# Twenty second-layer products of a fused Mamba-2 and ELU-MLP kernel done in halves of 128 tokens

## The chip, the cores and the metric

The kernel runs on one core of a Trainium2 chip. Its time is in device microseconds, the median of three runs; a profiled execution of its own gives the trace. Instructions run on five engines: PE (TensorE, matrix products; PEld is its weight loads), DVE (VectorE), ACT (ScalarE), POOL (GpSimd) and SP (SyncE, which here only issues transfers).

## The reference

A Mamba-2 scan in chunks, whose output is a batch of 3072 tokens of 256 numbers, goes through a two-layer MLP with ELU between. Inputs: x (4, 8, 768, 32), a (4, 8, 768), B and C (4, 8, 768, 16); the weights w_in (256, 2048) and w_out (2048, 256) are float64 arrays, the output is float32.

```
# scan, for each batch, head and chunk of 32 tokens (state: 16 x 32)
cum = cumsum(log(a));  M = (C B^T) * exp(cum_i - cum_j) * (i >= j)
y   = M x + exp(cum) * (C state)
state = exp(sum log a) * state + sum_j exp(cum_last - cum_j) B_j x_j
# bridge: heads side by side, 3072 tokens x 256
h = x @ w_in
g = where(h > 0, h, exp(min(h, 0)) - 1)
out = g @ w_out
```

## The kernel before, in words

The tokens are cut into 12 blocks (`n` = 0 to 11) of 256 (`BLK`), so that two neighbours, n and n+1 with n even, are the same stretch of two batches. The kernel works with chunks of 64 tokens (`Q`). The whole schedule is written out by hand: every engine carries out its instructions in the order in which the code issues them, and the loops at the end of the kernel interleave three kinds of work on PE.

The scan of a block consists of many small products in 32- or 64-wide corners of the array. `scores` (L532, C times B) and `sums` (L562, the sums for the states) stand one behind the other; some time later come `across` (L607, what the state at the start of a chunk gives) and `inside` (L626, M times x). For blocks 4 to 11 the scans of two blocks are issued together, so that `scores` and `sums` of a pair come as one run of small products and `across` and `inside` as another. `end_of_two` issues `across` and `inside` for blocks 4/5, 6/7, 8/9 and 10/11. The results of `inside` are copied out as yT, which feeds the first layer. `scan_ahead` and `turn_step` issue the scan's other parts: loads, exponentials, transposes.

The first layer of a pair of blocks (`front`, `mid`, `back`, all through `part_product`, L730) makes seven products in place of eight by a Strassen-like scheme on quarters of w_in, with sums on DVE (L747, L755, L763). Blocks 0 to 3 are done plainly (`l1`, L658). `elu` (L671, L678, L680) turns the results into g.

The second layer of blocks 0 and 1 is plain (`l2`, L779). For the pairs from 2/3 on `second(n)` makes seven products too. It is a generator: its caller draws some products at a time (`l2s`), between the first-layer products of the next pair. The 2048 hidden numbers are taken in two halves of four chunks; in each half r runs over the seven products, and for each r four products of a 128x128 weight quarter with a 128x256 piece of g add up in one PSUM tile (L869). DVE, ACT and POOL then add the tile to the parts of the output (`add`, L841; copies L875, L889; differences through `sub`, L795). For the last pair (`last`), g is the stationary operand and each product is done as two of 128 columns (L864); those of r = 6 in its second half stand at L849.

`second(4)`, for blocks 4 and 5, is drawn while the first layer of blocks 6 and 7 runs. After it come, in PE's order, `scores` and `sums` of blocks 8/9, `across` and `inside` of 8/9, then both for 10/11.

A product of float32 operands written as one in the code is two weight loads and two matmuls in the trace.

Of the kernel before, what the change touches and what calls it, by code (L numbers as in the profile page):

```python
# [16 lines left out]
P = 128  # L17
Q = 64
BLK = 2 * P
# [9 lines left out]
def kernel(  # L29
# [27 lines left out]
    nc = tc.nc  # L57
# [21 lines left out]
    def psum(shape, name):  # L79
        return p_a.tile(shape, F32, tag="a", name=name)  # L80
# [6 lines left out]
    for k in range(4):  # L87
        (nc.scalar if k % 2 else nc.sync).dma_start(
            out=la0[BH * k:BH * (k + 1)],
# [181 lines left out]
    for v in range(2):  # L271
        nc.gpsimd.affine_select(
            out=low16[Q * v:Q * v + Q], in_=low16[Q * v:Q * v + Q], pattern=[[1, Q]],
# [5 lines left out]
        out=hmask, in_=hmask, pattern=[[-N, NH]], compare_op=ALU.is_ge, fill=0.0,  # L279
        base=0, channel_multiplier=1)  # L280
    nc.gpsimd.affine_select(
        out=hmask, in_=hmask, pattern=[[N, NH]], compare_op=ALU.is_ge, fill=0.0,
# [8 lines left out]
        out=minus, in0=ident, scalar1=-1.0, scalar2=None, op0=ALU.mult)  # L291
# [474 lines left out]
    def row_of(n):  # L766
        b, g = place(n)
        return b * S + g * BLK
# [25 lines left out]
    def sub(out, in0, in1):  # L794
        nc.gpsimd.tensor_tensor(out=out, in0=in0, in1=in1, op=ALU.subtract)  # L795

    def quarters(n, i):


        A, B = g_of[n, i], g_of[n + 1, i]  # L800
        if n < 4:
            return A[:, 0], A[:, 1], B[:, 0], B[:, 1]
        return A[:, 0], B[:, 0], B[:, 1], A[:, 1]
# [5 lines left out]
    def sum_t2(n, half):  # L809
        for i in range(4 * half, 4 * half + 4):  # L810
            t2_of[n, i] = ffn.tile([P, BLK], F32, tag="t2", name="t2", bufs=4)
            b11, b21, b12, b22 = quarters(n, i)
            sub(t2_of[n, i], b22, b12)
# [3 lines left out]
    def second(n, last=False):  # L817


        c = c_of[n] = ffn.tile([P, 2, 2, 2, P], F32, tag="c", name="c_sum", bufs=1)  # L820
        c11, c12, c21, c22 = (
            c[:, at, :, e] if last else c[:, at, e] for e in range(2) for at in range(2))

        def finish(e, at):
            if last:
                return
            if (n, at) not in turned_of:
                turned_of[n, at] = conv.tile([P, 2, BLK], F32, tag="sgn", name="turned")
            nc.vector.transpose(
                out=turned_of[n, at][:, e], in_=c[:, at, e].rearrange("p t c -> p (t c)"))  # L830

        a11, a12, s1, a22 = a_out
        s2, s3, s4 = s_out
        for half in range(2):
            tmp = ffn.tile([P, 3, 2, P], F32, tag="tmp", name="p_sum", bufs=1)
            p1, p5, u = (tmp[:, r] for r in range(3))
            chunk = range(4 * half, 4 * half + 4)

            def add(out, in0, in1):
                eng = nc.vector if in0.tensor is ps.tensor else nc.gpsimd  # L840
                eng.tensor_tensor(out=out, in0=in0, in1=in1, op=ALU.add)  # L841

            for r, a in enumerate((a11, a12, s1, s2, s3, a22, s4)):
                if last and half and r == 6:
                    store(n, 0)
                    for ts, queue in enumerate((nc.scalar, nc.sync)):
                        ps = psum([P, P], "ps_o")
                        for i in chunk:
                            nc.tensor.matmul(  # L849
                                out=ps, lhsT=quarters(n, i)[3][:, ts * P:(ts + 1) * P],  # L850
                                rhs=a[:, i], start=(i == chunk[0]), stop=(i == chunk[-1]))
                        nc.vector.tensor_tensor(
                            out=c12[:, ts], in0=ps, in1=c12[:, ts], op=ALU.add)
                        r0 = row_of(n + 1) + ts * P
                        queue.dma_start(out=out[r0:r0 + P, 0:P], in_=c12[:, ts])
                    return
                pool, tag = (p_a, "a") if (7 * half + r) % 2 else (p_o, "o")
                ps = pool.tile([P, 2, P], F32, tag=tag, name="ps_o")
                for i in chunk:
                    b11, b21, b12, b22 = quarters(n, i)  # L860
                    b = (b11, b21, b12, t2_of[n, i], b11, b21, b22)[r]
                    if last:
                        for ts in range(2):
                            nc.tensor.matmul(  # L864
                                out=ps[:, ts], lhsT=b[:, ts * P:(ts + 1) * P], rhs=a[:, i],
                                start=(i == chunk[0] and ts == 0), stop=(i == chunk[-1]),
                                skip_group_check=True)
                    else:
                        nc.tensor.matmul(  # L869
                            out=ps.rearrange("p t c -> p (t c)"), lhsT=a[:, i], rhs=b,  # L870
                            start=(i == chunk[0]), stop=(i == chunk[-1]))
                    if i < chunk[-1]:
                        yield
                if r == 0:
                    nc.scalar.copy(out=p1, in_=ps)  # L875
                    for i in chunk:
                        b11 = quarters(n, i)[0]
                        sub(b11, t2_of[n, i], b11)
                    if half:
                        add(c11, c11, p1)  # L880
                elif r == 1:
                    add(c11, ps, c11 if half else p1)
                    if half:
                        finish(0, 0)
                    for i in chunk:
                        b21 = quarters(n, i)[1]
                        sub(b21, b21, t2_of[n, i])
                elif r == 2:
                    nc.scalar.copy(out=p5, in_=ps)  # L889
                elif r == 3:  # L890
                    add(u, ps, p1)
                    add(p5, p5, u)
                    if half:
                        add(c22, c22, p5)
                        add(c12, c12, p5)
                elif r == 4:
                    add(c22, ps, c22 if half else p5)
                    add(u, ps, u)
                    if half:
                        finish(1, 1)  # L900
                    if half:
                        add(c21, c21, u)
                    if last and half:
                        r0 = row_of(n + 1)
                        nc.sync.dma_start(
                            out=out[r0:r0 + BLK, P:2 * P].rearrange("(t p) c -> p t c", p=P),
                            in_=c22)
                    if not half:
                        sum_t2(n, 1)
                    elif n + 2 < NP:  # L910
                        sum_t2(n + 2, 0)
                elif r == 5:
                    add(c21, ps, c21 if half else u)
                    if half:
                        finish(1, 0)
                else:
                    add(c12, ps, c12 if half else p5)
                    if half:
                        finish(0, 1)
                yield  # L920

    def store(n, at):
        r0 = row_of(n + at)
        nc.sync.dma_start(
            out=out[r0:r0 + BLK, :].rearrange("(t p) e -> p t e", p=P),
            in_=c_of[n][:, at].rearrange("p t e c -> p t (e c)"))
# [29 lines left out]
    half = [slice(0, P), slice(P, 2 * P)]  # L956
# [272 lines left out]
    for n in range(4, NP, 2):  # L1229
        m = n + 2 if n + 2 < NP else None  # L1230
        steps = second(n - 2)

        def l2s(count):
# [10 lines left out]
        for k in range(16):  # L1244
            i = k // 2
# [55 lines left out]
    n = NP - 2  # L1301
    for k, _ in enumerate(second(n, True)):
        if k < 4:
            store_turned(n - 2, k // 2, k % 2)
# [30 lines left out]
```

## Time and profile before

| what | value |
| --- | --- |
| timed runs, us | 357.68, 359.85, 360.68; median 359.85 |
| profiled execution, us | 356.04 |
| its span, first to last instruction, us | 354.2 |
| granted TensorE clock, share of full speed | 1.00 |
| PE busy, us | 344.7 (97%) |
| DVE, ACT, POOL busy, us | 244.2, 204.1, 231.4 |
| instruction queue q8 | 28 packets, 0.46 MB |

The span leaves out what lies around the first and the last instruction of the program. A busy share is a mean over stages; PE's is near the whole. "x" and a number behind a group is a number of the trace's records. In lists of waits, "issue" is time in which an engine stood still and waited for nothing that the profile records.

### The profile page before, as it was taken

How to read it: one execution, taken by the hardware profiler on the slowest of the kernel's cores; microseconds unless marked ns; L12 is line 12 of the kernel's file. 1: busy time of each engine (PE TensorE's matmuls, PEld its weight loads, DVE VectorE, ACT ScalarE, POOL GpSimd, SP SyncE). 2: the span in 40 equal slices, each digit the busy share in tenths (PEclk: the TensorE clock that was granted, in tenths of full speed). 3: DMA queues.
4: the chain of work that ended last, by engine and by line, in shares of the span. 5: the costliest groups of instructions: out<-in, count | busy, mean ns of one | idle time of the engine just before them, and what ended most of it. 6: DMA issues, size and time to landing. Idle time of an engine off the chain costs nothing.

```text
span 354.2 us, 9156 instructions
## 1 busy us (share of the span) xinstructions
PE 344.7 (97%) x3510; PEld 297.0 (84%) x3510; DVE 244.2 (69%) x513; ACT 204.1 (58%) x497; POOL 231.4 (65%) x366
## 2 busy tenths in 40 slices
PE   8899999999999999999999998999998999999996
PEld 5679888888888888888888886888886888888996
DVE  4998978963999677776687774777683666567212
ACT  4789988886345567545666534577635443535100
POOL 5654555544486996985485986377786455455883
PEclk9999999999999999999999999999999999999999
DMA  8968997462351400267300268200000200000102
GB/s 152 270 172 204 291 219 173 115 100 43 69 130 38 84 1 0 34 132 144 55 0 2 31 129 158 45 3 0 7 9 5 44 2 0 0 17 15 32 0 61
DMA packets 87955, 26.45 MB, mean 75 GB/s; under 512 B 75048, under 2 KB 82792, under 8 KB 87912
## 3 DMA queue, kind: packets, MB, share of 16 engines
q1 hardware_dynamic: 85592, 25.60, 33.1%
q10 hardware_dynamic: 2320, 0.26, 0.5%
q8 instruction: 28, 0.46, 0.5%
q14 instruction: 15, 0.12, 0.1%
HBM read 22.51 MB, written 3.34 MB: 73 GB/s over the span
## 4 chain that ended last, share of the span: by engine, by line
PE 87%; DVE 3%; SPq 2%; issue 2%; POOL 2%; DMA 2%; ACT 1%; DVEq 0%; POOLq 0%; ACTq 0%
PE ps_h L730 26%; PE ps_o L869 25%; PE ps_h L658 15%; PE ps_o L779 8%; PE ps_o L864 7%; PE ps_y L626 2%; DMA w<-in_moe_w_in_dram 2%; PE ps_y L607 1%; PE ps_g L532 1%; PE ps_st L562 1%; POOL g L795 1%; SPq L169 1%; DVE g L680 1%; PE ps_o L849 1%; SPq L134 0%
## 5 line engine op out<-in xcount | busy, mean ns | idle before, releaser
L671 ACT ACTIVATE e<-ps_h 128x512 f32<-128x512 f32 x96 | 57.1, 594 | 90.4 <-DVE ps_h L755 48.5
L680 DVE SCALAR_TENSOR_TENSOR g<-e,ps_h 128x512 f32<-128x512 f32 x96 | 65.0, 679 | 13.9 <-ACT e L678 13.6
L869 PE MATMUL ps_o<-g,w_out 128*128 128x256 f32 x256 | 64.2, 380 | 0.0
L658 PE MATMUL ps_h<-yT,w_in 128*128 128x256 f32 (+1 forms) x272 | 60.4, 370 | 1.8 <-POOL w_in L239 1.8
L678 ACT ACTIVATE e<-e 128x512 f32<-128x512 f32 x96 | 61.0, 635 | 2.0
L807 POOL TENSOR_TENSOR g<-g 128x256 f32<-128x256 f32 x33 | 23.9, 726 | 53.8 <-DVE g L680 53.7
L658 PEld LDWEIGHTS ps_h<-yT,w_in 128*128 128x128 f32 x272 | 48.5, 190 | 9.1 <-POOL w_in L239 2.5
L869 PEld LDWEIGHTS ps_o<-g,w_out 128*128 128x128 f32 x256 | 48.4, 190 | 6.7
L512 ACT ACTIVATE L<-L,ncum 128x64 f32<-128x64 f32 x160 | 41.0, 337 | 0.2
L730 PE MATMUL ps_h<-y_sum,w_in 128*128 128x256 f32 x128 | 38.4, 381 | 0.2 <-DVE ps_h L755 0.2
L730 PE MATMUL ps_h<-yT,w_in 128*128 128x256 f32 x128 | 38.4, 381 | 0.0
L730 PE MATMUL ps_h<-y_sum,w_sum 128*128 128x256 f32 x128 | 38.1, 379 | 0.0
L763 DVE TENSOR_TENSOR ps_h<-ps_h,u_sum 128x512 f32<-128x512 f32 x32 | 22.3, 698 | 21.8 <-PE ps_h L730 21.6
L517 POOL TENSOR_SCALAR_AFFINE_SELECT L<-L 64x512 f32<-64x512 f32 x40 | 27.6, 689 | 11.8 <-ACT L L512 9.5
L747 DVE TENSOR_TENSOR u_sum<-ps_h,u_sum 128x512 f32<-128x512 f32 x32 | 22.1, 689 | 17.6 <-ACT u_sum L740 9.6
L869 PE MATMUL ps_o<-g,w_sum 128*128 128x256 f32 x128 | 33.2, 379 | 0.0
L779 PE MATMUL ps_o<-w_out,g 128*128 128x256 f32 x128 | 30.7, 382 | 0.0
L795 POOL TENSOR_TENSOR t<-g 128x256 f32<-128x256 f32 x40 | 28.9, 753 | 0.3
L755 DVE TENSOR_TENSOR ps_h<-ps_h,u_sum 128x256 f32<-128x256 f32 x32 | 13.8, 430 | 22.1 <-PE ps_h L730 22.1
L795 POOL TENSOR_TENSOR g<-g,t 128x256 f32<-128x256 f32 x40 | 28.8, 751 | 0.3
L795 POOL TENSOR_TENSOR g<-t,g 128x256 f32<-128x256 f32 x40 | 27.9, 729 | 1.1 <-PE ps_o L864 1.1
L730 PEld LDWEIGHTS ps_h<-y_sum,w_in 128*128 128x128 f32 x128 | 23.5, 189 | 4.9 <-DVE ps_h L755 1.2
(127 smaller groups left out, 586.1 us busy)
## 6 DMA issues: line engine op xcount, KB each, us to landing
L<-flat SPq DMA_DIRECT2D x20, 256.0 KB
w<-in_moe_w_out_dram SPq DMA_DIRECT2D x8, 512.0 KB
w<-in_moe_w_in_dram SPq DMA_DIRECT2D x7, 512.0 KB
xr<-in_x_dram SPq DMA_DIRECT2D x24, 128.0 KB
out_dram<-turned SPq DMA_DIRECT2D x64, 32.0 KB
bc<-in_B_dram SPq DMA_DIRECT2D x24, 64.0 KB
bc<-in_C_dram SPq DMA_DIRECT2D x22, 64.0 KB
ec<-flat_exp SPq DMA_DIRECT2D x10, 128.0 KB
```

The source lines that it names most:

```text
L512: nc.scalar.activation(L[:, h, u], L[:, h, u], ACT.Exp, bias=ncum[:, u, row:row + 1])
L517: nc.gpsimd.affine_select(out=part, in_=part, pattern=[[0, 4], [0, 2], [1, Q]], compare_op=ALU.is_ge, fill=0.0, base=0, channel_multiplier=-1)
L658: nc.tensor.matmul(out=ps[:, j, toks], lhsT=w_in[:, k, m * P:(m + 1) * P], rhs=yT[n // 2][:, k, n % 2].rearrange("p u i -> p (u i)")[:, toks],
L671: nc.scalar.activation(begun[0], lag[0][2], ACT.Relu, scale=-1.0)
L678: nc.scalar.activation(e, e, ACT.Exp, scale=-1.0)
L680: nc.vector.scalar_tensor_tensor(out=g_of[n, i], in0=e, scalar=1.0, in1=ps, op0=ALU.subtract, op1=ALU.max)
L730: nc.tensor.matmul(out=out, lhsT=lhsT, rhs=rhs, start=first, stop=True, skip_group_check=True)
L779: nc.tensor.matmul(out=o_of[n][:, ts], lhsT=g_of[n, j][:, m % 2, ts * P:(ts + 1) * P], rhs=w_out[:, m], start=(m == 0 and ts == 0), stop=( ...
L795: nc.gpsimd.tensor_tensor(out=out, in0=in0, in1=in1, op=ALU.subtract)
L807: eng.tensor_tensor(out=b12, in0=b12, in1=b11, op=ALU.subtract)
L864: nc.tensor.matmul(out=ps[:, ts], lhsT=b[:, ts * P:(ts + 1) * P], rhs=a[:, i], start=(i == chunk[0] and ts == 0), stop=(i == chunk[-1]), s ...
L869: nc.tensor.matmul(out=ps.rearrange("p t c -> p (t c)"), lhsT=a[:, i], rhs=b, start=(i == chunk[0]), stop=(i == chunk[-1]))
```

## The change

In `second`, for n = 4, in the first half and for r from 0 to 4, each of the four products over 256 token columns is made as two over 128 columns each, with the same weight quarter and into the two halves of the same PSUM tile. These are 20 products, which become 40. The first piece of the first chunk alone has the start flag; the second piece of that chunk has none. All other products pass through the new loop with a single cut that is the whole width.

```
--- before.py
+++ after.py
@@ -866,9 +866,14 @@
                                 start=(i == chunk[0] and ts == 0), stop=(i == chunk[-1]),
                                 skip_group_check=True)
                     else:
-                        nc.tensor.matmul(
-                            out=ps.rearrange("p t c -> p (t c)"), lhsT=a[:, i], rhs=b,
-                            start=(i == chunk[0]), stop=(i == chunk[-1]))
+                        cuts = [slice(0, BLK)]
+                        if n == 4 and not half and r < 5:
+                            cuts = [slice(0, P), slice(P, BLK)]
+                        for cut in cuts:
+                            nc.tensor.matmul(
+                                out=ps.rearrange("p t c -> p (t c)")[:, cut], lhsT=a[:, i],
+                                rhs=b[:, cut], start=(i == chunk[0] and cut.start == 0),
+                                stop=(i == chunk[-1]), skip_group_check=True)
                     if i < chunk[-1]:
                         yield
                 if r == 0:
```

## The prediction

> **What bounds the kernel now.** I read the page first. TensorE (PE) is busy for 97% of the span at the full granted clock and makes 87% of the chain that ended last, so only what shortens PE's own line of work counts. The page also has a queue that carries no data: q8 brings instructions, 28 packets.
>
> ```profile
> span 354.2 us, 9156 instructions
> PE 344.7 (97%) x3510; PEld 297.0 (84%) x3510; DVE 244.2 (69%) x513; ACT 204.1 (58%) x497; POOL 231.4 (65%) x366
> q8 instruction: 28, 0.46, 0.5%
> PE 87%; DVE 3%; SPq 2%; issue 2%; POOL 2%; DMA 2%; ACT 1%; DVEq 0%; POOLq 0%; ACTq 0%
> ```
>
> The list of PE's waits then says what PE lost, in us in total, times, and the longest:
>
> ```profile
> PE ps_y L626 <- issue: 3.1, 2, 1.5
> PE ps_h L658 <- POOL w_in L239: 1.8, 3, 1.0
> PE ps_idle L254 <- DVE idle L249: 1.1, 1, 1.1
> PE ps_h L730 <- DVE ps_h L755: 0.2, 1, 0.2
> PE ps_st L562 <- DVE g L680: 0.2, 1, 0.2
> ```
>
> The largest is not a wait for an engine: twice, inside `inside` (L626), PE stood for 1.5 us with nothing that the profile shows to wait for. PE's timeline places them: the bursts of small products (`across` L607, `inside` L626) of blocks 6/7, of 8/9 and of 10/11 (columns: start us, us, what, and in brackets the idle time before it).
>
> ```profile
> 159.29 0.83 PE L607 MATMUL ps_y<-cts,Sx 32*64 32x64 f32 x48
> 160.05 1.51 PE L626 MATMUL ps_y<-M,xr 64*32 64x64 f32 x128
> 161.49 0.70 PE L730 MATMUL ps_h<-yT,w_in 128*128 128x256 f32 x2
> ...
> 212.97 0.91 PE L607 MATMUL ps_y<-cts,Sx 32*64 32x64 f32 x64
> 213.81 1.37 PE L626 MATMUL ps_y<-M,xr 64*32 64x64 f32 x114
> 216.72 0.34 PE L626 MATMUL ps_y<-M,xr 64*32 64x64 f32 x14 [1.53 <-issue]
> ...
> 268.02 0.91 PE L607 MATMUL ps_y<-cts,Sx 32*64 32x64 f32 x64
> 268.86 1.15 PE L626 MATMUL ps_y<-M,xr 64*32 64x64 f32 x91
> 271.54 0.63 PE L626 MATMUL ps_y<-M,xr 64*32 64x64 f32 x37 [1.54 <-issue]
> ```
>
> The same work runs through in one burst, stops after 114 of 128 matmuls in the next and after 91 in the third: the stop belongs to no fixed place of the work. What it belongs to shows in the transfers. The DMA view of 214.3 to 214.4 us holds one instruction packet, that of 269.1 to 272 us another:
>
> ```profile
> q8 instruction: 1, 0.02, 62.6%
> ...
> q8 instruction: 1, 0.02, 2.1%
> ```
>
> The packet records put their starts at 214.34 and 269.18 us. PE resumes 2.38 and 2.36 us later: it had run out of instructions.
>
> **Where the edges lie.** I number PE's entries of the trace (weight loads, matmuls, recorded semaphore instructions) in order of start: 7116. With 28 packets and 0.46 MB that is about 255 entries and 16 KB a packet. The first late entry is 5058 in the burst of 8/9 and 6081 in that of 10/11; 1023 apart, the packets being the 19th and the 23rd: four blocks of 255.75. So edges lie near 4293, 4548, 4803, 5058, 5314, 5569, 5825, 6081 and 6336, and the packet for one block starts when PE is about one block ahead of it. A burst of `across` and `inside` has 384 entries (96 products, each two weight loads and two matmuls) and takes 2.3 us; wide products take 108 ns an entry, 27 us a block. Only a block that lies wholly in small products can be eaten before the next is there. Before, the bursts are entries 4701 to 5085 and 5770 to 6154: blocks 4803 to 5058 and 5825 to 6081 lie wholly inside them. For blocks 6/7 (3632 to 3984) edges lie near 3528, 3783 and 4038, the last beyond the end, and nothing is lost.
>
> **The change, part by part.** It removes 20 products of 256 columns (first half, r from 0 to 4, chunks 0 to 3, n = 4) and adds 40 of 128. Nothing else differs: the other engines' instructions stand in the same order, no transfer or wait is added, and the accumulations of L841 and the copies of L875 and L889 still start at the last product of a group.
>
> *The split itself.* A wide product is two matmul entries, at 216 ns from start to start; the last stage runs the same products as 128 columns (L864). The chain of waits has both:
>
> ```profile
> 197.15 1.73 PE ps_o L869 x8
> 326.32 23.23 PE ps_o L864 x208
> ```
>
> 1.73/8 = 0.216 us, so 0.432 per wide product; 23.23/208 = 0.1117, so 4 x 0.1117 = 0.447 per pair. 20 x 0.015 = +0.30 us, on PE's path, as PE has no idle time from 163 to 182 us where they run. Less than nothing is excluded: the same columns stream. The dear bound is a weight load that hides behind nothing:
>
> ```profile
> L869 PEld LDWEIGHTS ps_o<-g,w_out 128*128 128x128 f32 x256 | 48.4, 190 | 6.7
> ```
>
> At 190 ns for each of four entries it is 20 x (0.760 - 0.432) = +6.6 us. I take 0.30, since L864 is the same product in the same form.
>
> *The shift.* 40 products for 20 are 80 more entries ahead of all later work. The edges stay; the bursts move to 4781 to 5165 and 5850 to 6234. The burst of 10/11 now starts 25 entries after edge 5825, and its next edge, 6081, is 231 entries in. The packet for 6081 is asked for some 50 entries of wide work before the burst, about 5 us, more than it needs: the 1.54 us go. The edge after, 6336, lies 102 wide entries (11 us) beyond the burst: no new stop.
>
> The burst of 8/9 is the doubtful one. Edges 4803 and 5058 are 22 and 277 entries in, so one whole block still lies inside. In wide work a packet starts when PE begins an entry 269 to 283 short of the edge that it serves (nine packets, edges 255 apart: 275, 276, 276, 269, 283, 279, 272, 279, 280; mean 277), because the instruction reader runs ahead of the array. For 5058 that is entry 4781, the very start of the burst. PE reaches entry 277 of the burst 1.58 us after its start (both bursts above), the instructions are there 2.37 us after the packet's start: 2.37 - 1.58 = 0.79 us of stop. Against that, the ten entries ahead of a burst took 1.5 to 1.9 us, not 1.1 (the first small weight load waits for the end of a wide product and for POOL, 0.33), so the packet gains some 0.4 to 0.8 us. I take 0.5 us left of 1.53. Bounds: 0, and 1.53 if the reader runs ahead less; seven entries of scatter are 0.75 us.
>
> *Scores and sums* (L532, L562; 256 entries in 2.2 us) move to 4414 to 4674 and 5515 to 5742. Edges in them, 4548 and 5569, are followed by the next at 129 and 83 wide entries past the end, 9 us or more. Nothing is added; a block fitting exactly there would cost 0.2 us (2.37 - 2.2) or somewhat more.
>
> *What may be late next.* With the stops gone, do other engines hold PE back? From 110 to 163 us, the same loop without a stop, PE was busy 52.80 of 53.00 us with DVE at 38.74; from 217 to 272 us with the stop DVE was at 38.40. They kept up with the shorter stretch already; the cover gone might bring a wait like the 0.25 us of L730 for L755 at 211.9, which I price at nothing. Stores and loads follow 1.5 to 2.3 us earlier, on a queue with 13% of the DMA time in use from 217 us on.
>
> *Sum,* on the profiled execution (356.04 us, span 354.2): -1.53 + 0.5 - 1.54 + 0.30 = -2.27, so 353.8. The median of the timed runs, 359.85, lies 3.8 above the profiled one; on it, 357.6.
>
> [...] The trace shows PE dry 118 entries after a packet starts, so no more than about two blocks are held. [...]
>
> **Rivals.** (1) Edge 5058 still stops the first burst for its full 1.53 us: -1.54 + 0.30, so 358.6. For it: a whole block still lies in the burst. Against: the packet is asked for in slow work now. (2) On the other side: the stop belongs to the burst and not to the edges (something in the late blocks' operands): both stay, +0.30, 360.2, slower than before. Against: the 255.75 spacing, and the clean burst at 160. (3) The halves' weight loads don't hide: 359.85 - 2.57 + 6.6 = 363.9. It decides from 140 ns per entry on ((2.57/20 + 0.432)/4); against it the 111.7 of L864. (4) The timed runs' extra 3.8 us hold longer stops than the profile shows; if half of it does, 357.6 - 1.9 = 355.7. For it only that gap.
>
> **How the numbers follow.** Forecast 0.60, with its own range 356.5 to 358.4 (the left-over stop from 0 to 1.3 and the medians' scatter); rival 1 0.17, rival 2 0.08, rival 3 0.04, rival 4 0.11. The single runs before spread over 3 us (357.68 to 360.68), so a median is uncertain by about one. The range runs from 355.8, which reaches into rival 4, to 360.0, which takes in rival 1 and the early half of rival 2's scatter; rival 3 is left out. A change under 1% (3.6 us) is about what a measurement of this kernel can't tell from none, and the forecast is 0.6%: same 0.75. Faster: rival 4 and the forecast's tail, 0.18. Slower: rival 3 and rival 2's tail, 0.07.
>
> **What would show it.** PE's waits after should have no issue idle in the burst of 10/11, and under 1 us in that of 8/9, 277 entries in (after about 75 of L626's 128 matmuls); the split products should stand at 112 ns per entry; q8 should still have 28 packets. I am wrong if 1.5 us stops stand in both bursts, if a stop appears in L532 or L562, or if PE's waits for L755 grow to a microsecond.

## The result, and the profile after

The changed kernel takes 356.92 us (median of 20 runs, 355.09 to 359.39), the kernel before 359.30 (20 runs, 357.30 to 362.83). The ratio is 0.9927, 95% interval 0.9903 to 0.9951: 2.4 us less, between 1.8 and 3.5. The forecast was 357.6.

The page of the profiled execution after shows none of that gain: its span is longer.

```profile
span 355.6 us, 9236 instructions
PE 347.2 (98%) x3550; PEld 300.0 (84%) x3550; DVE 243.6 (69%) x513; ACT 204.1 (57%) x497; POOL 231.2 (65%) x366
q8 instruction: 28, 0.46, 0.5%
```

There are 80 more entries (40 weight loads, 40 matmuls) and as many instruction packets. PE's waits (us in total, times, longest) have one stop where there were two, but a longer one:

```profile
PE ps_y L626 <- issue: 2.0, 1, 2.0
PE ps_h L658 <- POOL w_in L239: 1.8, 3, 0.8
PE ps_idle L254 <- DVE idle L249: 1.1, 1, 1.1
PE ps_h L730 <- DVE ps_h L755: 0.2, 1, 0.2
PE ps_st L562 <- DVE g L680: 0.2, 1, 0.2
```

PE's timeline shows where: the burst of 10/11 runs through, that of 8/9 stops after 74 matmuls of L626.

```profile
214.13 0.91 PE L607 MATMUL ps_y<-cts,Sx 32*64 32x64 f32 x64
214.98 0.99 PE L626 MATMUL ps_y<-M,xr 64*32 64x64 f32 x74
217.92 0.94 PE L626 MATMUL ps_y<-M,xr 64*32 64x64 f32 x54 [1.96 <-issue]
218.79 1.22 PE L730 MATMUL ps_h<-yT,w_in 128*128 128x256 f32 x2
219.81 1.06 PE L730 MATMUL ps_h<-y_sum,w_sum 128*128 128x256 f32 x2
...
271.21 0.91 PE L607 MATMUL ps_y<-cts,Sx 32*64 32x64 f32 x64
272.05 1.51 PE L626 MATMUL ps_y<-M,xr 64*32 64x64 f32 x128
```

The two pairs of L730 after the stop take 1.22 and 1.06 us, where the same two take 0.70 and 0.59 at the full clock (the changed kernel with the spreads moved, at 218.87 and 219.41 us). The table by windows says why (after the window: its length, then busy time and count of PE, PEld, DVE, ACT, POOL; then the granted clock, DMA share, GB/s):

```profile
214.13:218.79 4.66, 2.70 (x193) 2.31 (x192) 1.29 (x2) 1.89 (x6) 2.50 (x4) 0.95 0.66 146
218.79:222.50 3.71, 3.71 (x12) 3.07 (x11) 0.67 (x2) 2.00 (x5) 2.09 (x3) 0.60 0.80 145
222.50:271.21 48.71, 48.65 (x328) 41.80 (x326) 36.43 (x76) 28.24 (x73) 33.80 (x52) 1.00 0.09 15
```

After the stop the clock was halved; the clock records put it at 0.5 from 218.34 us for 3.413 us, and half of that, 1.7 us by estimate, is lost. The profiled execution of before had no such drop, and it had reached the burst of 6/7, ahead of all split products, 0.88 us earlier (159.29 against 160.17). That is why two single profiles mislead here, and why the comparison goes by the timed runs, each of which has its granted clock.

### The profile page after: what moved, and what is told of

Same layout as the page of the kernel before. It is cut to its first block, busy times and chain, and to the rows that moved or that the text cites. A ratio compares the mean times of both kernels' runs of the same rounds, so it can differ in the third digit from the quotient of the medians.

```text
span 355.6 us, 9236 instructions
## 1 busy us (share of the span) xinstructions
PE 347.2 (98%) x3550; PEld 300.0 (84%) x3550; DVE 243.6 (69%) x513; ACT 204.1 (57%) x497; POOL 231.2 (65%) x366
## 4 chain that ended last, share of the span: by engine, by line
PE 88%; DMA 3%; DVE 3%; SPq 2%; issue 2%; POOL 1%; ACT 1%; DVEq 0%; POOLq 0%; ACTq 0%
PE ps_h L730 26%; PE ps_o L873 25%; PE ps_h L658 14%; PE ps_o L779 8%; PE ps_o L864 7%; PE ps_y L626 2%; DMA w<-in_moe_w_in_dram 2%; PE ps_y L607 1%; PE ps_g L532 1%; PE ps_st L562 1%; DMA bc<-in_C_dram 1%; POOL g L795 1%; SPq L169 1%; DVE g L680 1%; SPq L111 1%
## 5 line engine op out<-in xcount | busy, mean ns | idle before, releaser
L873 PE MATMUL ps_o<-g,w_out 128*128 128x256 f32 (+1 forms) x280 | 64.5, 363 | 0.0
L873 PEld LDWEIGHTS ps_o<-g,w_out 128*128 128x128 f32 x280 | 50.2, 191 | 6.5
L730 PE MATMUL ps_h<-y_sum,w_in 128*128 128x256 f32 x128 | 38.9, 385 | 0.2 <-DVE ps_h L755 0.2
L730 PE MATMUL ps_h<-yT,w_in 128*128 128x256 f32 x128 | 38.9, 386 | 0.0
L730 PE MATMUL ps_h<-y_sum,w_sum 128*128 128x256 f32 x128 | 38.5, 383 | 0.0
L873 PE MATMUL ps_o<-g,w_sum 128*128 128x256 f32 (+1 forms) x136 | 33.2, 367 | 0.0
L730 PEld LDWEIGHTS ps_h<-y_sum,w_in 128*128 128x128 f32 x128 | 23.6, 191 | 4.8 <-DVE ps_h L755 1.2
```

The source lines that it names most:

```text
L730: nc.tensor.matmul(out=out, lhsT=lhsT, rhs=rhs, start=first, stop=True, skip_group_check=True)
L873: nc.tensor.matmul(out=ps.rearrange("p t c -> p (t c)")[:, cut], lhsT=a[:, i], rhs=b[:, cut], start=(i == chunk[0] and cut.start == 0), st ...
```

## The experiments

"Stop" is the idle time that the timeline gives. The runs of before that belong to the three groups of experiments gave medians of 359.56, 359.07 and 359.55.

**Is it the split?** The same twenty products of a pair behind all bursts:

```
-                        if n == 4 and not half and r < 5:
+                        if n == 8 and not half and r < 5:
```

> The same twenty products are split in the pair 8/9 instead of 4/5, behind all bursts, so no burst moves. Theory A: both stops stay, after 114 and 91 matmuls of L626, and the time is before plus 0.30, about 359.6 us. Rival B (the split products themselves are what gains): 356.9 us like the change.

Measured: 359.64 us, ratio 1.0015 (0.9977 to 1.0053). Both stops stand at the matmuls where they were before:

```profile
214.85 1.37 PE L626 MATMUL ps_y<-M,xr 64*32 64x64 f32 x114
217.78 0.34 PE L626 MATMUL ps_y<-M,xr 64*32 64x64 f32 x14 [1.55 <-issue]
...
269.92 1.15 PE L626 MATMUL ps_y<-M,xr 64*32 64x64 f32 x91
272.85 0.63 PE L626 MATMUL ps_y<-M,xr 64*32 64x64 f32 x37 [1.79 <-issue]
```

The splitting itself gains nothing.

**Half the shift.** Ten products, 40 entries:

```
+                        if n == 4 and not half and r < 5 and i % 4 < 2:
```

> Ten products are split, 40 entries added: the bursts of 8/9 and 10/11 start at 4741 and 5810, and in both a whole block still lies inside (edge entries 62 and 317, 15 and 271 of the burst). Theory A: two stops, after about 94 and 71 matmuls of L626, and no gain: 359.3 + 0.15 = 359.5 us, from 358.5 to 360.5. Rival C (the gain grows with the shift or with the number of split products): half of 2.4, 358.1 us.

Measured: 358.37 us, ratio 0.9972 (0.9943 to 1.0000). The places are those expected to the matmul, 94 and 71, the lengths are not:

```profile
215.09 1.18 PE L626 MATMUL ps_y<-M,xr 64*32 64x64 f32 x94
218.45 0.54 PE L626 MATMUL ps_y<-M,xr 64*32 64x64 f32 x34 [2.18 <-issue]
...
272.42 0.95 PE L626 MATMUL ps_y<-M,xr 64*32 64x64 f32 x71
274.16 0.80 PE L626 MATMUL ps_y<-M,xr 64*32 64x64 f32 x57 [0.79 <-issue]
```

The time fell by 1.2 us, as theory C had it and not A. The two stops went different ways. In 10/11 the edge before the stop lies 15 entries in, and the packet started 0.11 us ahead of the burst's first product; with that edge 55 entries in (before) it started 1.17 us behind. In 8/9 the edge moved from 102 entries in to 62, and yet the packet came later, 1.69 us behind the first product and not 1.37, and the stop was longer. So a stop shrinks when the edge before it stands close to the burst's start, but not in step with the shift. My expectation had treated a stop as there or not.

**A whole block.** 64 products, 256 entries: the first-layer products of 6/7 for i below 4 are split in `part_product` as well.

```
+                        if n == 4 and 7 * half + r < 9:
...
+            split_l1[:] = [1] if n == 6 and i < 4 else []
```

> Sixty-four products are split (36 of the second layer of 4/5, 28 of the first layer of 6/7), 256 entries, one whole block: the bursts stand to the edges as in the kernel before. Theory A: two stops again, after 114 and 91 matmuls of L626 give or take two, and before plus 64 x 0.015, about 360.3 us. Rival C (any shift, or more splitting, gains): 356.9 us or less.

Measured: 360.21 us, ratio 1.0001 (0.9968 to 1.0033). Both stops are back at the same matmuls, 114 and 91, though everything there stands 256 entries later:

```profile
215.20 1.37 PE L626 MATMUL ps_y<-M,xr 64*32 64x64 f32 x114
218.73 0.34 PE L626 MATMUL ps_y<-M,xr 64*32 64x64 f32 x14 [2.16 <-issue]
...
272.66 1.15 PE L626 MATMUL ps_y<-M,xr 64*32 64x64 f32 x91
275.34 0.63 PE L626 MATMUL ps_y<-M,xr 64*32 64x64 f32 x37 [1.54 <-issue]
```

The stops depend on the place of the burst modulo one block. Theory C falls here.

**The mirror.** 50 products, 200 entries: 8/9 should be freed and 10/11 stopped.

```
+                        if n == 4 and 7 * half + r < 9:
...
+            split_l1[:] = [1] if n == 6 and i < 2 else []
```

> Fifty products are split (36 of the second layer of 4/5, 14 of the first layer of 6/7): 200 entries more. The burst of 8/9 starts at 4901, with edges 98 entries ahead of it and 157 in; that of 10/11 at 5970, with edges 110 and 366 in. Theory A: the stop of 8/9 goes, since the packet for 5058 is asked for some ten microseconds before the burst, ahead of any wait at its start, and a stop of 1.5 to 2.2 us stands in the burst of 10/11 after about 118 matmuls of L626. 359.5 - 1.53 - half a clock drop + 0.75 = 357.8 us. Rival B (a stop belongs to its burst): 8/9 still stops.

Measured: 357.89 us, ratio 0.9967 (0.9942 to 0.9991).

```profile
215.43 1.51 PE L626 MATMUL ps_y<-M,xr 64*32 64x64 f32 x128
...
268.84 1.41 PE L626 MATMUL ps_y<-M,xr 64*32 64x64 f32 x119
272.32 0.32 PE L626 MATMUL ps_y<-M,xr 64*32 64x64 f32 x9 [2.08 <-issue]
```

8/9 runs clean, 10/11 stops at 119 where 118 was worked out. No stop belongs to its burst.

**Both bursts clean, at first sight.** 32 products, 128 entries:

```
+                        if n == 4 and 7 * half + r < 8:
```

> Thirty-two products are split instead of twenty, so 128 entries are added and the last two across/inside bursts start at entries 4829 and 5898: no block of about 255 entries lies wholly in either. Theory A (a block eaten before the next arrives; a stop of about 2 us then also halves the granted clock for 3.4 us in some executions, 1.7 us): no issue idle in PE's waits, granted clock 1.00 throughout, and 356.9 - 2.0 - 0.85 + 0.18 = 354.2 us, with less scatter than before. Rival B (the gain comes from the split products themselves, and the stops belong to the bursts): 32/20 of the gain of 2.4, 355.5 us, with the stop in the burst of 8/9 still there.

Measured: 355.94 us, ratio 0.9911 (0.9874 to 0.9948), a miss: a stop of 1.36 us stayed in 8/9.

```profile
215.46 0.74 PE L626 MATMUL ps_y<-M,xr 64*32 64x64 f32 x50
217.56 1.04 PE L626 MATMUL ps_y<-M,xr 64*32 64x64 f32 x78 [1.36 <-issue]
```

The edge was again entry 5058. But its packet started at 214.69 us, 0.07 after the burst's first product, although the edge ahead lies 26 entries before it. In the changed kernel the burst of 10/11 has an edge 25 entries ahead, and there the packet came 2.1 us before the burst. What differs is the DMA engines:

```profile
212.00:213.50 1.50, 1.33 (x7) 0.82 (x5) 1.50 (x5) 0.00 (x0) 1.26 (x2) 1.00 1.09 227
213.50:214.60 1.10, 1.04 (x4) 0.68 (x4) 0.01 (x1) 1.03 (x2) 1.10 (x3) 1.00 1.06 216
...
268.00:270.00 2.00, 2.00 (x51) 1.35 (x53) 0.78 (x3) 1.23 (x2) 2.00 (x4) 1.00 0.02 4
```

Share 1.09 and 1.06 before 8/9, 0.02 around 10/11 (in the changed kernel 0.00 and 0.04 from 267 to 271 us). SP's timeline names the traffic:

```profile
209.90 2.41 SPq L375 DMA_DIRECT2D L<-flat  x4
212.36 0.63 SPq L383 DMA_DIRECT2D ec<-flat_exp  x1
213.03 4.16 SPq L937 DMA_DIRECT2D out_dram<-turned  x4
```

**The spreads moved.** The kernel with 32 splits, and the four spreads of `flat` for blocks 10 and 11 behind the second `ec` load in SP's order:

```
-        if 4 < m < NP and n % 2 == 1 and i in (4, 5):
+        if 4 < m < NP and m != 10 and n % 2 == 1 and i in (4, 5):
             spread_cum(m + i - 4)
...
                 spread_exp(m + i)
+                if m == 10 and i == 1:
+                    spread_cum(10)
+                    spread_cum(11)
```

> The kernel with thirty-two split products, in which the four spreads of flat for blocks 10 and 11 (256 KB each) are issued after the second ec load instead of ahead of the first, so the DMA engines are idle or nearly so while the packet for edge 5058 is asked for. In the kernel with thirty-two splits that packet started at 214.69 us, at the burst's first product, though the edge before it lies 26 entries ahead of the burst, and 1.36 us were lost. Theory D (the packet waited behind data in the DMA engines, whose share was over 1.0 from 212 to 216 us): the packet starts 3 to 5 us before the burst, no stop, and about 1.4 us less than with the spreads early, 354.4. Rival H (the instruction reader is held by the semaphore waits at the start of the burst, L730 for DVE and L607 for POOL, and asks late): the packet still starts within half a microsecond of the burst's first product, a stop of 1.2 to 2 us stays, and the time is the same, 355.9.

Measured: 353.69 us, ratio 0.9861 (0.9831 to 0.9891), the fastest version. The packet starts at 211.79 us, 2.03 ahead of the burst, not 3 to 5, but about as far ahead as in 10/11 of the changed kernel. PE's waits hold no issue any more, and none of its four runs lost clock:

```profile
PE ps_h L658 <- POOL w_in L239: 1.6, 3, 0.8
PE ps_idle L254 <- DVE idle L249: 1.1, 1, 1.1
PE ps_h L730 <- DVE ps_h L755: 0.2, 1, 0.2
PE ps_st L562 <- DVE g L680: 0.2, 1, 0.2
```

Rival H falls for this kernel, where the edge lies ahead of the burst: the same semaphore waits stand at the burst's start.

**The spreads moved alone.** The same edit on the kernel before.

> The kernel before with the spreads late and nothing split. Theory D with the edges: the packet is asked for from inside the burst in any case, so both stops stay, after 114 and 91 matmuls of L626, that of 8/9 at 1.2 to 1.8 us; 358.7 us, from 358 to 359.5. Rival G (the late spreads gain by themselves, through fewer collisions of transfers with the engines' work): 357 us or less with both stops in place.

Measured: 360.82 us, ratio 1.0050 (1.0018 to 1.0082): slower, which neither expected.

```profile
215.00 1.42 PE L626 MATMUL ps_y<-M,xr 64*32 64x64 f32 x114
219.86 0.34 PE L626 MATMUL ps_y<-M,xr 64*32 64x64 f32 x14 [3.44 <-issue]
```

The stop doubled. The late spreads are issued from 212.4 to 215.1 us, and with the 1.37 us of before the packet would have started just behind them, by estimate at 215.53 us. It started 2.96 us after the burst's first product, at 217.12, and all 12 runs lost clock. Late spreads gained nothing alone: they helped where the packet started ahead of them (211.79 us against 213.37, with 32 splits) and harmed here, where it started behind them.

**On the change itself.** The same edit on the changed kernel.

> The changed kernel (twenty split products) with the four spreads of flat for blocks 10 and 11 issued after the second ec load. Theory D (the residual stop of 1.96 us was longer than the forecast's 0.5 because the packet for edge 5058 waited behind those spreads): the packet starts within half a microsecond of the burst's first product instead of 1.02 us behind it, the stop shrinks to between 0.3 and 1.2 us, few executions lose clock, and the time is 356.9 - 1.2 - 0.8 = 354.9 us. Rival P (only the place of the edge counts, 22 entries into the burst): the stop stays at 1.7 to 2.2 us and the time at 356.9.

Measured: 355.89 us, ratio 0.9925 (0.9888 to 0.9961). The packet started 0.93 us after the burst's first product, and the stop was 2.19 us; D's numbers failed. The spreads had been moved onto the packet (issued from 212.7 to 215.4 us, its start 215.08), and the packet itself took 1.60 us in place of 1.40. Beside the kernel before, the gain is that of the change alone (0.9925 and 0.9927). The stop is in P's range, but as the data had not been moved out of the way, the run doesn't tell D from P.

**Cover in place of a shift.** The kernel before, four wide products drawn between `across` and `inside`:

```
-            inside(across(*ns), *ns)
+            y = across(*ns)
+            if cover:
+                cover[0](4)
+            inside(y, *ns)
...
                     end_of_two(n, k)
-                    l2s(2)
+                    if not (n in (6, 8) and i in (6, 7)):
+                        l2s(2)
...
+        cover[:] = [l2s] if n in (6, 8) else []
```

> Nothing is split, no entry is added: the kernel before, in which four wide products of the second layer, drawn two from the step before and two from the step after, stand between across and inside of blocks 8/9 and 10/11. The edges fall in the bursts as before, but the block between them holds 16 wide entries, 1.73 us, more than the stops of 1.53. Theory A: no stop or one under 0.4 us in either, no clock drop there, and 359.5 - 3.07 - about 1.4 (0.76 drops per run at 1.9) = 355.1 us, from 354 to 356.5 if the moved products bring small waits for DVE. Rival E (what a stop costs is hidden anyway by what follows, or the moved products leave DVE latency bare at the steps they come from): 358 us or more, with new waits of PE for DVE.

Measured: 355.88 us (six runs, none with a clock drop), ratio 0.9918 (0.9892 to 0.9944). 10/11 is clean; in 8/9 1.41 us stayed, its packet starting 3.0 us after the burst's first product. No new wait for DVE appeared around the moved products, so E falls. With the spreads late as well:

> No split; four wide products between across and inside of blocks 8/9 and 10/11, and the spreads late. With the spreads early the stop of 8/9 stayed at 1.41 us, its packet starting 3.0 us after the burst's first product. Theory D: the packet comes about 1 to 1.5 us earlier, the stop is at most 0.4 us, none in 10/11, no clock drop, 355.9 - 1.4 = 354.5 us. Rival H (the reader asks late, whatever the DMA engines do): 1.4 us stay, 355.9.

Measured: 356.23 us, ratio 0.9926 (0.9896 to 0.9957), stop 1.65 us, packet again 3.0 us behind: a miss for theory D. Rival H's figures lie nearer. But the spreads (212.7 to 215.6 us) were issued just ahead of the packet (some 216.5 us) again, so the run doesn't decide between the two.

**Second profiles** of the unchanged two:

> The kernel before once more, for a second profile: stops after 114 and 91 matmuls of L626 again, each between 1.3 and 2.2 us, if they belong to the edges; elsewhere if they are chance.

> The changed kernel once more, for a second profile: one stop, in the burst of 8/9 after 74 matmuls of L626, between 1.5 and 2.2 us if the late packet is the rule and near 0.5 us if the first profile was chance.

Before: stops of 1.82 us after 114 matmuls and 1.80 after 91. After: one of 1.79 us after 74. Places repeat; lengths vary by some tenths.

```profile
214.74 1.37 PE L626 MATMUL ps_y<-M,xr 64*32 64x64 f32 x114
217.94 0.34 PE L626 MATMUL ps_y<-M,xr 64*32 64x64 f32 x14 [1.82 <-issue]
...
270.07 1.15 PE L626 MATMUL ps_y<-M,xr 64*32 64x64 f32 x91
273.02 0.63 PE L626 MATMUL ps_y<-M,xr 64*32 64x64 f32 x37 [1.80 <-issue]
```

## Why the prediction was right, and where it was not

*Bound and edges: right.* Edges at fixed entries of the stream explain every stop, in thirteen of fourteen profiles (that of 32 splits with the spreads moved has none), to the matmul or one beside it: 114/91, 94/71, 119, 74, 50. Rival 2 (a stop belongs to its burst) fell with the change itself, where 10/11 runs clean, and with the mirror, where 8/9 does. One sentence was too narrow: only a block wholly in small products can be eaten too early. With 32 splits the block began 26 entries ahead of the burst, its packet came 2.1 us later than it could, and PE ran dry.

*The split: right.* From the first product of burst 6/7 to that of 8/9 it is 53.68 us in both profiles of before, 53.96 and 53.98 in those of the change: +0.28 and +0.30 against 0.30. Rival 3 (weight loads that don't hide) is out.

*10/11: right, its size too small.* I counted 1.54 us, the idle time. From the start of the last matmul before the stop to the start of the next it is 1.75 us, since the list of waits counts from that matmul's modelled end. In the second profile of before it is 2.01. Mean gain 1.88. The margin was smaller than I wrote: the packet started 2.11 and 2.21 us ahead of the burst, not about 5, and PE reached the edge 1.34 us into the burst.

*8/9: the term that failed.* I forecast 0.5 left of 1.53; 1.96 and 1.79 were left, outside my upper bound. The raw estimate was 2.37 - 1.58 = 0.79 with the packet at the burst's start. In fact the packet started 1.02 and 1.04 us after it, and the instructions came 2.77 and 2.58 us after the packet's start. The step that failed is the lead of 277 entries: I had read it in wide work and took it over, as a number of entries, to the start of a burst, and then took another 0.3 us off.

In time, the packets of my nine rows started 0.9 to 2.8 us ahead of PE's first entry behind the edge before the one they serve. Inside a burst that lead is gone. In the eight profiles in which the edge before lies 55 entries or more inside the burst of 10/11, the packet started 0.8 to 0.95 us after PE had begun that entry (0.95 twice in before). In the burst of 8/9 of the changed kernel, with the edge 22 entries in, it was 0.93 and 0.95.

The data transfers are not needed to explain this. The DMA engines were busy ahead of 8/9 (share 0.96 to 1.17) and almost idle around 10/11 (0.03), and the packet was as late in both (first two lines: after, up to and behind the first product of 8/9; third: before, 10/11):

```profile
213.50:214.10 0.60, 0.60 (x4) 0.28 (x2) 0.00 (x0) 0.57 (x2) 0.60 (x2) 1.00 1.17 317
214.10:216.00 1.90, 1.86 (x139) 1.60 (x138) 1.29 (x2) 1.00 (x3) 1.81 (x3) 1.00 0.96 201
...
268.00:270.00 2.00, 2.00 (x156) 1.77 (x156) 1.28 (x2) 1.11 (x3) 1.79 (x3) 1.00 0.03 8
```

The slower arrival need not be a sign of data either: in the second profile of before the instructions came 2.62 us after the packet's start in 10/11, at a DMA share of 0.06 or less. The transfers ahead of 8/9 are missing from my sum, though, and a part of theirs is not excluded, since no run has the edge 22 entries in and idle DMA engines. Why the lead is lost stays open too. With the edge 15 entries in (ten products, 10/11) the packet still came ahead of the burst; a reader held by the wait of the burst's first product (rival H) would fit both, but no run tests it. Rival 1, the full stop in 8/9, describes the profile better than my forecast does.

*What made up for it.* The stop's other price, which I had only as half of rival 4. Of 80 runs of before, 50 lost clock, 61 drops by the clocks' size; of 20 runs of the change 10, with 11 drops. The runs of before without a drop have a median of 357.77 us, those with one 359.62, which is close to the 1.7 us of a half-rate stretch. So the median of 359.85 stood 3.8 above the profile of 356.04 partly for want of a drop there, and not mainly for its short stops: of the 1.46 us by which the second profile of before, without a drop too, is longer (357.50), 0.55 lie in the two stops, and 0.93 had passed when the burst of 6/7 began. Fewer drops are worth (0.76 - 0.55) x 1.7 = 0.36 us.

Sum by the runs: -1.88 (10/11), +0.20 (8/9, from a mean of 1.88 to 2.08 from start to start), +0.30 (split), -0.36 (drops): -1.7 us, against -2.4 measured (-3.5 to -1.8). Among runs without a drop the medians differ by 357.77 - 355.74 = 2.0, of which 1.4 is accounted for. The rest, some 0.6 us, stays open; two profiles of each kernel are few for stops whose lengths vary by 0.3, and these two medians come from different sets of runs.

The right total thus came partly from an error (8/9) against terms too small (10/11, the drops).

## What to carry to other kernels

An idle stretch that waits for "issue" inside a run of very small instructions is worth laying beside the instruction queue's packets: number the engine's entries, find the spacing of the edges, and a few tens of entries more or less ahead of it will tell. Price the stop by time and not by entries: in the six stops of before and the changed kernel, 3.2 to 3.7 us passed from PE's first entry behind one edge until it had the instructions behind the next, and a whole block of small products lasts 1.5 us (255.75 of a burst's 384 entries, which take 2.3 us). So a block that lies wholly inside a burst left 1.7 to 2.2 us of stop, and moving it within the burst by 80 entries saved nothing; only an edge close to the burst's start or ahead of it did.

Then look at what the DMA engines carry ahead of the packet's start: moving a transfer out of its way brought the kernel with 32 splits from 355.94 to 353.69 us (timed in separate groups of runs, the latter in four; against the kernel before in each group, 0.9911 and 0.9861), and moving it to just ahead of the packet in the kernel before cost 1.3 us (359.55 to 360.82). And count a stop from start to start, with the clock that it may cost afterwards; one profile can show neither.

## What the runs showed of the hardware

Instruction packets started later with data transfers in their way: with the DMA share at 1.09 and 1.06 ahead of the burst the packet for the same edge started 2.1 us later than with the spreads out of its way (32 splits; 0.57 and 0.36 from 210 to 213.5 us), and in the kernel before 1.6 us later with them issued just ahead of it (2.96 against 1.37 us after the burst's start), one profile each. A high share alone did not do it: in 8/9 of before, at 0.99, the packet started 0.83 us after PE began the entry behind the edge, no later than with nearly idle DMA engines (0.95 us in 10/11, at 0.03).

Behind a stop of about 2 us PE's clock can halve: in the changed kernel's profile, behind the stop of 1.96 us, it stood at 0.5 for 3.413 us. In the profiles the stops of 1.79 us (with the split behind all bursts), 1.96, 2.08, 2.16, 2.18 and 3.44 us were followed by a drop; 2.19 us once was not, nor any other of 1.82 or less. Each stood within a burst of small products of some 2 us, and no run tells the stop's part from the burst's; after bursts without a stop no drop followed (in the changed kernel the clock stood at 1.00 from the burst of 10/11 on, 271.21 to 326 us).
